# Attention beside a token-mixing MLP: where the last MLP products run, how wide token mixing's first weights are read, and how the first weights are loaded

## The chip, the cores and the metric

The kernel runs on one core of one Trainium2 chip. That core has a matrix engine (TensorE, "PE" in the profile, with its weight loads shown apart as "PEld"), a vector engine (VectorE, "DVE"), a scalar engine (ScalarE, "ACT"), GpSimd ("POOL"), and a sync engine (SyncE, "SP") that here only issues DMAs. Each engine works through its own queue in order; between engines there are semaphores. Matrix products land in PSUM, eight banks of 128 partitions by 512 fp32 numbers, and other engines carry them from there to SBUF.

The metric is device microseconds (us) for one execution, lower is better. A kernel's time is the median of its executions; one more execution is taken under the profiler, and its trace is what this document reads.

## What is computed

From the reference, cut to what matters (S = 2048 tokens, D = 448 features, H = 16 query heads of Dh = 28, one key and one value head, F = 1792):

```python
x = A_x
g = sigmoid((x * gate_w).sum(-1, keepdims=True))

# a: attention, 16 query heads on one key and one value head
q = (x @ wq) in 16 heads;  k = x @ wk;  v = x @ wv
p = softmax(q @ k.T * Dh ** -0.5)
a = concat_heads(p @ v) @ wo

# b: token mixing, then a channel-mixing MLP
h  = gelu(layernorm(x) @ w1)                # 448 -> 448
hs = the four quarters of h, shifted by +1, -1, +2, -2 tokens, @ w2
x1 = x + hs
b  = x1 + gelu(layernorm(x1) @ w3) @ w4     # 448 -> 1792 -> 448

out = g * a + (1 - g) * b
```

## The kernel before

**Stages.** The program runs in this order: (1) queries, keys, values and gate, as one product with the padded weights `wq` (512 columns), written to DRAM as `qd`; (2) token mixing, `stage_w1` and `stage_w2` for four blocks of 512 tokens; (3) the channel MLP, for each block 14 slices of 128 of the 1792 hidden features (`w3_part`, `w4_part`); (4) attention, for 16 units `u` (a block of 512 queries and four heads), each in eight stretches `v` of 256 keys, 128 stretches `k = 8u + v` in all; (5) a tail. Tiles and engines' orders are written by hand: each engine gets its instructions in the order of the Python code, so a line that is moved in the code moves in the queues.

**Accuracy by splitting.** A product in fp32 is made of products in a faster form (fp32r): weights and data are split in a high and a low part (`w1h`, `w1l`; `ah`, `al`), and high×high, high×low and low×high are added up in PSUM. In `proj` (L129 to L135) this makes 11 matmuls for the 448 input features: three chunks of 128 with three products each, and a last chunk with two.

**The start.** The scalar engine's queue issues the loads of `wqraw`, the sync queue those of the first block of `x` (`xkv_0`), both in four chunks of 128 features. Chunk 0 of `wqraw` comes in two DMAs, columns 0 to 127 and 128 to 511. Meanwhile PE runs 20 matmuls on zeros (L93). `first_queries` then takes chunk 0 of weights and data unsplit in fp32 (L312, four matmuls which the trace shows as eight passes), and chunks 1 to 3 in split form (L316), for which ACT casts `wqh` (L97) and DVE makes `wql` (L98).

**Token mixing's w1.** `stage_w1(b)` makes the four quarters of `h`, each with one `proj` call. The weights of quarter `m` are 112 columns, `w = slice(m * C, (m + 1) * C)` with `C = 112`, so that 112 of 128 PSUM partitions are written. DVE multiplies `ps[0:C]` by the layernorm factor, ACT applies gelu.

**The last MLP slice.** In the last block (tokens 1536 to 2047, x1 tiles n = 12 to 15), slice 13's products with `w4` are not made in the MLP. They are put off into attention: `last_g` holds the slice's gelu (`gh_late`, `gl_late`), and `w4_half` makes, for 128 tokens and 224 of 448 columns, three matmuls into one bank, whose sum DVE multiplies by `gi` (that is 1 - g) and adds to `x1`, which POOL has already multiplied by `gi` (`weigh_x1`, L642, in the POOL queue ahead of attention). There are eight halves, one in each of the stretches k = 3 to 10 (`W4_AT = 3`).

**A stretch of attention.** For stretch k, PE makes the scores of 2 × 128 keys (`scores`, L896: four heads side by side in the array's rows, 12 matmuls into four banks, twice). `exps` takes six of the eight banks by ACT (L920, exp from PSUM) and two by DVE (L917, a plain copy to `pd`); `late_exps` lets ACT do the exp of those two at once (L925). Then PE makes what is slotted in (a `w4_half`, or from the unit's fourth stretch on a `wo_half` of an earlier unit), and `values(k-1)` (L936: 32 matmuls into two banks), which DVE adds to `o`. Banks are handed out from a list in turn: `take` removes the first, and whoever has read a bank puts it at the end. A matmul that gets a bank waits until its last reader is done. One `values` lags one stretch behind the scores.

Of the kernel before, what the change touches and what calls it, by code (L numbers as in the profile page):

```python
# [42 lines left out]
def gated_mix_kernel(  # L43
# [85 lines left out]
    def proj(ps, wh, wl, ah, al):  # L129
        for c in range(3):  # L130
            nc.tensor.matmul(ps, wh[:, c, :], ah[:, c, :], start=(c == 0), stop=False)  # L131
            nc.tensor.matmul(ps, wh[:, c, :], al[:, c, :], start=False, stop=False)  # L132
            nc.tensor.matmul(ps, wl[:, c, :], ah[:, c, :], start=False, stop=False)  # L133
        nc.tensor.matmul(ps, wh[:, 3, :], ah[:, 3, :], start=False, stop=False)  # L134
        nc.tensor.matmul(ps, wl[:, 3, :], ah[:, 3, :], start=False, stop=True)  # L135
# [114 lines left out]
    with tc.tile_pool(name="s1b", bufs=1) as s1b, \  # L250
# [25 lines left out]
        wql = s1.tile([P, 4, 512], F32R, name="wql")  # L276
        xraw[0] = s1.tile([P, 4, 512], F32, tag="raw", bufs=3, name="xkv_0")
        for c in range(4):
            for cols in (slice(0, P), slice(P, 512)) if c == 0 else (slice(0, 512),):
                nc.scalar.dma_start(wqraw[:, c, cols], wq[:, c, cols])  # L280
            nc.sync.dma_start(xraw[0][:, c, :], xT[:, c, 0:512])
        nc.scalar.activation(first, powt, AF.Gelu_apprx_tanh)
        w1h = s1.tile([P, 4, D], F32R, name="w1h")
        w1l = s1.tile([P, 4, D], F32R, name="w1l")
        w2h = s1b.tile([P, 4, D], F32R, name="w2h")
        w2l = s1b.tile([P, 4, D], F32R, name="w2l")
        hh, hl, acts = {}, {}, {}
# [135 lines left out]
        def stage_w1(b, between=None):  # L423
# [6 lines left out]
                    nc.gpsimd.tensor_copy(tt[b][0:C, :, 0:2], f32(tt[b - 1])[0:C, :, 512:514])  # L430
            for i, m in enumerate(ORDER):
                ps = mm1(f"h_{b}_{m}")
                w = slice(m * C, (m + 1) * C)
                proj(ps[0:C, :], w1h[:, :, w], w1l[:, :, w], *xact[b])
                if between:
                    between(i)
                hf = s1.tile([P, 512], F32, tag="hf", bufs=3, name=f"hf_{b}_{m}")
                nc.vector.tensor_mul(hf[0:C, :], ps[0:C, :], rb_of[b][0:C, :])
                nc.scalar.activation(hh[b][0:C, m, 2:514], hf[0:C, :], AF.Gelu_apprx_tanh)
                nc.scalar.activation(hf[0:C, :], hf[0:C, :], AF.Gelu_apprx_tanh)  # L440
                nc.gpsimd.tensor_tensor(hl[b][0:C, m, 2:514], hf[0:C, :], f32(hh[b])[0:C, m, 2:514],
                                        ALU.subtract)
                if i == 1:
                    carry_h(b)
# [50 lines left out]
        centre_w1()  # L495
        stage_q(7)
        stage_q(8)
        split_w_high(w1raw, w1h, w1l)
        for t in range(4):
            ln1_tile(1, t)  # L500
        split_w_low(w1raw, w1h, w1l)
        stage_q(9)
        ln1_send(0)
        ln1_read(0)
# [248 lines left out]
    with tc.tile_pool(name="s3", bufs=1, reuse_waits="tile") as s3, \  # L753
# [77 lines left out]
            t, h = divmod(i, 2)  # L831
            wo_job(u, t, None, slice(224 * h, 224 * h + 224))

        weigh_x1(NT - 4, NT)

        def w4_half(i):
            t, h = divmod(i, 2)
            n = NT - 4 + t
            cols = slice(224 * h, 224 * h + 224)
            tok = slice(t * P, (t + 1) * P)  # L840
            gh, gl = last_g
            ps = bank(f"job_{n}_{h}")[:, cols]
            nc.tensor.matmul(ps, gh[:, tok], w4h[-1][:, 1, cols], start=True, stop=False)
            nc.tensor.matmul(ps, gh[:, tok], w4l[-1][:, 1, cols], start=False, stop=False)
            nc.tensor.matmul(ps, gl[:, tok], w4h[-1][:, 1, cols], start=False, stop=True)
            nc.vector.scalar_tensor_tensor(x1[:, n, cols], ps, gi[:, n:n + 1], x1[:, n, cols],
                                           op0=ALU.mult, op1=ALU.add)

        def redo_unit(i, acc, gd):
            b, g = i // NG, i % NG  # L850
# [95 lines left out]

        READ = (0, 3, 1, 2)
        DRAIN = 3
        W4_AT = 3

        for k in range(NU * NV):
            u, v = divmod(k, NV)
# [6 lines left out]
            for kt in (2 * v, 2 * v + 1):  # L959
                exps(u, kt, scores(u, kt))  # L960
            late_exps(u, v)
            if 0 <= k - W4_AT < 8:
                w4_half(k - W4_AT)
            if v >= 4 and u:
                wo_half(u - 1, v - 4)
            if v < 4 and u > 1:
# [156 lines left out]
```

## Time and profile before

| | before |
|---|---|
| median of 3 executions | 922.65 us (922.6 to 924.09) |
| the profiled execution's own time | 921.51 us |
| its span in the trace | 919.7 us |
| granted TensorE clock, mean | 0.998 |
| PE busy | 910.3 us, 99% of the span |
| ACT busy | 634.8 us, 69% |
| DVE busy | 543.7 us, 59% |
| POOL busy | 104.9 us, 11% |

The profiled execution's time is 1.8 us above the span, which is what lies around the instructions, and 1.1 us under the median. "Busy" counts an instruction from start to end; matmuls overlap each other, so a busy PE is not one at its peak, and what a matmul costs is read from the distance between starts. In a timeline row, the first number is the start in us from the span's start, the second the duration, then engine, line, operation, output<-input, shape and count; in brackets stands the idle time ahead of it and what ended that.

### The profile page before, as it was taken

The page shows a single profiled execution, that of the slowest core. Times are in us where ns is not written, and L with a number is a line of the kernel's source. Part 1 is how long each engine was busy: PE and PEld are TensorE (multiplying, and loading weights), DVE is VectorE, ACT ScalarE, POOL GpSimd, SP SyncE. Part 2 cuts the span into 40 slices and gives each one's busy share as a digit, 9 for nine tenths or more (in the row PEclk, how much of TensorE's full clock was granted, in tenths as well). Part 3 has the DMA queues.
Part 4 walks back from the last instruction along what each step waited for, and adds up shares of the span by engine and source line. Part 5 has one row for each costly group of instructions (what it writes and reads, how often), then busy time and mean ns, then how long its engine had stood idle before and what let it go on. Part 6 is the DMA issues. An engine that isn't in the chain of part 4 may idle for free.

```text
span 919.7 us, 24031 instructions
## 1 busy us (share of the span) xinstructions
PE 910.3 (99%) x10051; PEld 646.7 (70%) x10051; DVE 543.7 (59%) x1085; ACT 634.8 (69%) x1134; POOL 104.9 (11%) x135
## 2 busy tenths in 40 slices
PE   9999999999999999999999999999999999999997
PEld 6788888888888888875655665666665556666563
DVE  4675264631435746446666766666667666676664
ACT  5542255322222131259999999999999999999994
POOL 2143200221000530031000000000000000000000
PEclk9999999999999999999999999999999999999999
DMA  8821543220222132110100001000011000110001
GB/s 289 301 77 43 165 144 118 40 66 21 41 69 50 33 97 65 28 55 22 26 26 2 26 14 55 25 26 26 10 39 46 26 4 25 35 45 3 14 14 43
DMA packets 41953, 51.82 MB, mean 56 GB/s; under 512 B 9328, under 2 KB 27824, under 8 KB 41840
## 3 DMA queue, kind: packets, MB, share of 16 engines
q1 hardware_dynamic: 38672, 44.77, 17.0%
q10 hardware_dynamic: 3168, 5.47, 1.7%
q8 instruction: 80, 1.31, 0.6%
q14 instruction: 33, 0.27, 0.1%
HBM read 37.04 MB, written 11.93 MB: 53 GB/s over the span
## 4 chain that ended last, share of the span: by engine, by line
PE 96%; ACT 1%; DMA 1%; DVE 0%; issue 0%; ACTq 0%; DVEq 0%
PE bank L936 23%; PE bank L896 22%; PE bank L816 7%; PE acc L678 5%; PE acc L677 5%; PE acc L679 5%; PE g L132 4%; PE g L131 4%; PE g L133 4%; PE hs L456 1%; PE hs L457 1%; PE g L134 1%; PE g L135 1%; PE h L131 1%; PE h L132 1%; PE h L133 1%
## 5 line engine op out<-in xcount | busy, mean ns | idle before, releaser
L920 ACT ACTIVATE p<-bank 128x512 f32<-128x512 f32 x768 | 390.2, 619 | 4.8 <-PE bank L896 4.4
L936 PE MATMUL bank<-p,vext 128*32 128x256 f32 x3072 | 243.9, 379 | 0.8 <-ACT p L920 0.8
L936 PE MATMUL bank<-pd,vext 128*32 128x256 f32 x1024 | 242.2, 379 | 0.3 <-ACT pd L925 0.3
L917 DVE COPY pd<-bank 128x512 f32<-128x512 f32 x256 | 176.5, 691 | 53.2 <-PE bank L896 52.1
L936 PEld LDWEIGHTS bank<-p,vext 128*32 128x32 f32 x3072 | 125.1, 110 | 82.3 <-ACT p L920 2.1
L667 ACT ACTIVATE gh<-g 128x512 fp32r<-128x512 f32 x55 | 32.8, 597 | 186.7 <-PE g L135 186.7
L941 DVE TENSOR_TENSOR o<-o,bank 128x256 f32<-128x256 f32 x222 | 93.4, 421 | 91.4 <-ACT p L920 49.9
L925 ACT ACTIVATE pd<-pd 128x1024 f32<-128x1024 f32 x128 | 142.2, 1111 | 0.0
L896 PE MATMUL bank<-qh,kH 30*128 30x512 f32 x1024 | 119.8, 444 | 0.0
L936 PEld LDWEIGHTS bank<-pd,vext 128*32 128x32 f32 x1024 | 111.6, 110 | 1.3 <-ACT pd L925 0.7
L669 DVE TENSOR_TENSOR gl<-gf,gh 128x512 fp32r<-128x512 f32 x55 | 37.9, 688 | 123.7 <-ACT gf L668 123.7
L896 PE MATMUL bank<-qh,kL 28*128 28x512 f32 x1024 | 106.2, 394 | 0.0
L896 PE MATMUL bank<-ql,kH 28*128 28x512 f32 x1024 | 105.6, 389 | 0.0
L896 PEld LDWEIGHTS bank<-qh,kH 30*128 30x128 f32 x1024 | 61.0, 182 | 58.2 <-ACT p L920 47.0
L678 PE MATMUL acc<-w4l,gh 128*128 128x448 f32 x220 | 80.4, 366 | 0.0
L677 PE MATMUL acc<-w4h,gh 128*128 128x448 f32 x220 | 80.3, 365 | 0.0
L679 PE MATMUL acc<-w4h,gl 128*128 128x448 f32 x220 | 80.1, 364 | 0.0
L816 PE MATMUL bank<-wof,on 128*32 128x224 f32 (+1 forms) x992 | 73.1, 370 | 0.3 <-ACT p L920 0.3
L132 PE MATMUL g<-al,w3h 128*128 128x512 f32 x168 | 65.8, 392 | 0.0
L131 PE MATMUL g<-ah,w3h 128*128 128x512 f32 x168 | 65.6, 391 | 0.0
L133 PE MATMUL g<-ah,w3l 128*128 128x512 f32 x168 | 65.5, 390 | 0.0
L896 PEld LDWEIGHTS bank<-ql,kH 28*128 28x128 f32 x1024 | 52.6, 185 | 8.2
(196 smaller groups left out, 1165.2 us busy)
## 6 DMA issues: line engine op xcount, KB each, us to landing
qd<-qf ACTq DMA_DIRECT2D x16, 256.0 KB
qm<-qd SPq DMA_DIRECT2D x16, 256.0 KB
qr<-qd SPq DMA_DIRECT2D x16, 256.0 KB
rb<-rd SPq DMA_DIRECT2D x15, 256.0 KB
x<-in_x_dram SPq DMA_DIRECT2D x4, 896.0 KB
xd<-xt SPq DMA_DIRECT2D x16, 224.0 KB
w34raw<-in_w_dram SPq DMA_DIRECT2D x7, 512.0 KB
out_dram<-ot SPq DMA_DIRECT2D x15, 224.0 KB
```

Source lines behind the costliest of these rows:

```text
L131: nc.tensor.matmul(ps, wh[:, c, :], ah[:, c, :], start=(c == 0), stop=False)
L132: nc.tensor.matmul(ps, wh[:, c, :], al[:, c, :], start=False, stop=False)
L133: nc.tensor.matmul(ps, wl[:, c, :], ah[:, c, :], start=False, stop=False)
L677: nc.tensor.matmul(ps, gh[:, tok], w4h[i][:, k, :], start=(f == 0), stop=False)
L678: nc.tensor.matmul(ps, gh[:, tok], w4l[i][:, k, :], start=False, stop=False)
L679: nc.tensor.matmul(ps, gl[:, tok], w4h[i][:, k, :], start=False, stop=(f == stop))
L816: nc.tensor.matmul(ps[32 * j:32 * j + 32, cols], on_of[u][:, tok], wof[:, g, cols], start=True, stop=True, tile_position=(0, 32 * j))
L896: nc.tensor.matmul(bs[j], w, a, start=(i == 0), stop=(i == 2), tile_position=(32 * j, 0))
L917: nc.vector.tensor_copy(ps[j], bs[j])
L920: behind[kt % 2] = nc.scalar.activation(ps[j], bs[j], AF.Exp, scale=SCALE)
L925: ins = nc.scalar.activation(pd, pd, AF.Exp, scale=SCALE)
L936: nc.tensor.matmul(pv[32 * j:32 * j + 32, q], vext[:, kt, :], p_of[u, kt][j][:, q], start=(kt % 2 == 0), stop=(kt % 2 == 1), tile_position ...
```

## The change

```diff
@@ loads of the first weights
         for c in range(4):
-            for cols in (slice(0, P), slice(P, 512)) if c == 0 else (slice(0, 512),):
-                nc.scalar.dma_start(wqraw[:, c, cols], wq[:, c, cols])
+            nc.scalar.dma_start(wqraw[:, c, :], wq[:, c, :])
             nc.sync.dma_start(xraw[0][:, c, :], xT[:, c, 0:512])
         nc.scalar.activation(first, powt, AF.Gelu_apprx_tanh)
-        w1h = s1.tile([P, 4, D], F32R, name="w1h")
-        w1l = s1.tile([P, 4, D], F32R, name="w1l")
+        w1h = s1.tile([P, 4, D + P - C], F32R, name="w1h")
+        w1l = s1.tile([P, 4, D + P - C], F32R, name="w1l")
+        for w in (w1h, w1l):
+            nc.gpsimd.memset(f32(w)[:, :, D:D + P - C], 0.0)
@@ stage_w1
-                w = slice(m * C, (m + 1) * C)
-                proj(ps[0:C, :], w1h[:, :, w], w1l[:, :, w], *xact[b])
+                w = slice(m * C, m * C + P)
+                proj(ps, w1h[:, :, w], w1l[:, :, w], *xact[b])
@@ the split of w1
-        split_w_high(w1raw, w1h, w1l)
+        split_w_high(w1raw, w1h[:, :, 0:D], w1l[:, :, 0:D])
...
-        split_w_low(w1raw, w1h, w1l)
+        split_w_low(w1raw, w1h[:, :, 0:D], w1l[:, :, 0:D])
@@ attention
-        weigh_x1(NT - 4, NT)
-
-        def w4_half(i):
-            t, h = divmod(i, 2)
+        def w4_job(t):
             n = NT - 4 + t
-            cols = slice(224 * h, 224 * h + 224)
             tok = slice(t * P, (t + 1) * P)
             gh, gl = last_g
-            ps = bank(f"job_{n}_{h}")[:, cols]
-            nc.tensor.matmul(ps, gh[:, tok], w4h[-1][:, 1, cols], start=True, stop=False)
-            nc.tensor.matmul(ps, gh[:, tok], w4l[-1][:, 1, cols], start=False, stop=False)
-            nc.tensor.matmul(ps, gl[:, tok], w4h[-1][:, 1, cols], start=False, stop=True)
-            nc.vector.scalar_tensor_tensor(x1[:, n, cols], ps, gi[:, n:n + 1], x1[:, n, cols],
-                                           op0=ALU.mult, op1=ALU.add)
+            ps = bank(f"job_{n}")[:, 0:D]
+            nc.tensor.matmul(ps, gh[:, tok], w4h[-1][:, 1, :], start=True, stop=False)
+            nc.tensor.matmul(ps, gh[:, tok], w4l[-1][:, 1, :], start=False, stop=False)
+            nc.tensor.matmul(ps, gl[:, tok], w4h[-1][:, 1, :], start=False, stop=True)
+            nc.vector.tensor_add(x1[:, n, :], x1[:, n, :], ps)
...
-        W4_AT = 3
...
             late_exps(u, v)
-            if 0 <= k - W4_AT < 8:
-                w4_half(k - W4_AT)
+            if k == 0:
+                for t in range(3):
+                    w4_job(t)
+            if k == 1:
+                w4_job(3)
+                weigh_x1(NT - 4, NT)
```

So there are three edits. Chunk 0 of `wqraw` comes in one DMA in place of two. Each quarter of `w1` is read with the 16 columns behind it (the next quarter's, or, for the last, zeros that POOL writes once), and the 16 extra rows of the result are not used. The eight half jobs of stretches 3 to 10 become four whole jobs, three in stretch 0 and one in stretch 1; their sums are added to `x1` unweighted, and POOL's weighting of these four tiles comes after them.

How this moves the engines' queues, at three places. On ACT, the queue's head (loads of `wqraw` are issued from here), before:

```order
L280 DMA wqraw<-in_wq_dram 128x128
L280 DMA wqraw<-in_wq_dram 128x384
L280 DMA wqraw<-in_wq_dram 128x512 x3
L282 ACT_TABLE_LOAD
L282 ACTIVATE first<-powt 128x4
```

and with the change:

```order
L279 DMA wqraw<-in_wq_dram 128x512 x4
L281 ACT_TABLE_LOAD
L281 ACTIVATE first<-powt 128x4
L122 CAST ahk_145<-xkv_120 128x512
L97 CAST wqh<-wqraw 128x512
```

One issue fewer stands ahead of the table load and the first casts. On PE, at the start of attention, from the end of the second set of scores (`kH` and `kL` are the keys' parts, `qh` and `ql` the queries', a bank's number is its tile), before:

```order
L896 MATMUL bank_3508<-ql_1030,kH 128x512
L896 MATMUL bank_3509<-ql_1030,kH 128x512
L896 MATMUL bank_3502<-qh_1029,kH 128x512
L896 MATMUL bank_3505<-qh_1029,kH 128x512
L896 MATMUL bank_3503<-qh_1029,kH 128x512
L896 MATMUL bank_3504<-qh_1029,kH 128x512
```

and with the change:

```order
L892 MATMUL bank_3509<-ql_1031,kH 128x512
L892 MATMUL bank_3510<-ql_1031,kH 128x512
L840 MATMUL bank_3503<-w4h_1480,gh_late 128x448
L841 MATMUL bank_3503<-w4l_1481,gh_late 128x448
L842 MATMUL bank_3503<-w4h_1480,gl_late 128x448
L840 MATMUL bank_3506<-w4h_1480,gh_late 128x448
L841 MATMUL bank_3506<-w4l_1481,gh_late 128x448
L842 MATMUL bank_3506<-w4h_1480,gl_late 128x448
L840 MATMUL bank_3504<-w4h_1480,gh_late 128x448
L841 MATMUL bank_3504<-w4l_1481,gh_late 128x448
L842 MATMUL bank_3504<-w4h_1480,gl_late 128x448
L892 MATMUL bank_3505<-qh_1030,kH 128x512
```

The nine matmuls of three jobs stand between the second and the third set of scores; the jobs take the three banks that come free first (of the first scores' heads 0, 3 and 1), and the third scores begin with the next. On DVE, at the same place, with the change (before, the four rows of L843 are not here; eight rows of L846, one a stretch, follow later):

```order
L913 COPY pd_3533<-bank_3506 128x512
L913 COPY pd_3533<-bank_3510 128x512
L843 TENSOR_TENSOR x_72<-x_72,bank_3503 128x448
L843 TENSOR_TENSOR x_72<-x_72,bank_3506 128x448
L843 TENSOR_TENSOR x_72<-x_72,bank_3504 128x448
L913 COPY pd_3534<-bank_3508 128x512
L913 COPY pd_3534<-bank_3504 128x512
L843 TENSOR_TENSOR x_72<-x_72,bank_3505 128x448
```

The adds of three jobs stand between the copies of the first and of the second stretch. On POOL the four weightings of `x1` keep their place in the order, ahead of the split of unit 1's queries, but now wait for these adds.

## The prediction

> **What bounds the kernel now.** I read the page first (busy shares, then the chain of waits), then busy time by windows at the places that the change touches, then the timelines there.
>
> ```profile
> PE 910.3 (99%) x10051; PEld 646.7 (70%) x10051; DVE 543.7 (59%) x1085; ACT 634.8 (69%) x1134; POOL 104.9 (11%) x135
> PE 96%; ACT 1%; DMA 1%; DVE 0%; issue 0%; ACTq 0%; DVEq 0%
> core 0: us, PE busy (x) PEld busy (x) DVE busy (x) ACT busy (x) POOL busy (x), PEclk, DMA share, GB/s
> 0.00:5.20 5.20, 4.15 (x20) 2.97 (x21) 0.17 (x1) 0.41 (x1) 2.50 (x14) 1.00 0.62 161
> 37.50:58.00 20.50, 20.50 (x91) 15.41 (x91) 13.02 (x19) 12.59 (x21) 7.73 (x8) 1.00 0.55 170
> 404.40:415.85 11.45, 10.65 (x144) 6.23 (x144) 5.92 (x11) 11.44 (x22) 5.56 (x6) 1.00 0.42 130
> 415.85:448.33 32.48, 32.16 (x476) 19.69 (x472) 21.01 (x42) 32.05 (x57) 3.69 (x4) 1.00 0.07 16
> ```
>
> PE is 99% busy and 96% of the chain that ended last. Token mixing (37.5 to 58) has no PE gap: what PE saves there comes off the end. In attention two engines are full at once: from 404.4 to 415.85 ACT is busy for 11.44 of 11.45 us and PE is not, from 415.85 to 448.33 both nearly. So each stage has its own price, and I take the three edits in the order in which they run.
>
> **First weights whole.**
>
> ```profile
> 0.73 4.03 ACTq L280 DMA_DIRECT2D wqraw<-in_wq_dram  x5
> 5.08 0.33 PEld L312 LDWEIGHTS q<-xkv,wqraw 128*128 128x128 f32 x2
> 6.28 0.30 PEld L312 LDWEIGHTS q<-xkv,wqraw 128*128 128x128 f32 x2 [0.88 <-DMA wqraw<-in_wq_dram]
> 7.67 0.19 PEld L312 LDWEIGHTS q<-xkv,wqraw 128*128 128x128 f32 x1 [0.24 <-issue]
> 8.10 0.19 PEld L312 LDWEIGHTS q<-xkv,wqraw 128*128 128x128 f32 x1 [0.24 <-issue]
> 8.55 0.62 ACT L97 CAST wqh<-wqraw 128x512 fp32r<-128x512 f32 x1 [1.75 <-DMA wqraw<-in_wq_dram]
> 9.22 0.77 PEld L316 LDWEIGHTS q<-ahk,wqh 128*128 128x128 f32 x4 [0.93 <-ACT wqh L97]
> ```
>
> The eight fp32 passes step by 0.43 us (7.67 to 8.10). Two run on the narrow piece, then PE stands until the other 384 columns are there at 6.28. The last pass begins at 8.53 and would let PE go on at 8.96; but chunk 1 lands only at 8.55, and PE resumes at 9.22. Now the issues are one fewer, so chunks 1 to 3 are asked for earlier. Does chunk 0 make it by 5.2, when PE's warm-up ends? By the window's row 161 GB/s × 5.2 us = 837 KB are in by then; chunk 0 of weights and of data are 2 × 262 = 524 KB, and both are first in their queues. I take yes. Then eight passes run without a stop, 5.2 + 8 × 0.43 + 0.05 = 8.7, and chunk 1, asked for one issue earlier, is cast by then. Gain 9.22 − 8.7 = 0.5 us. The other end: the whole chunk lands when the second piece did, 6.28 + 8 × 0.43 + 0.1 = 9.82, a loss of 0.6. Behind this PE is without gaps, so either passes through.
>
> **w1 in 128 columns.** 16 quarters × 11 = 176 matmuls, each with its load.
>
> ```profile
> L131 PEld LDWEIGHTS h<-ahk,w1h 128*112 128x112 f32 x48 | 8.4, 174 | 2.7 <-issue 0.2
> L131 PEld LDWEIGHTS q<-ahk,wqh 128*128 128x128 f32 x36 | 6.8, 188 | 1.7 <-issue 0.2
> 16.65 0.39 PE L131 MATMUL q<-ahk,wqh 128*128 128x512 f32 x1
> 24.13 0.91 PE L397 MATMUL wsum_ps<-wsum,ones 128*128 128x448 f32 x2
> 25.12 0.40 PE L132 MATMUL q<-alk,wqh 128*128 128x512 f32 x1
> 27.43 0.39 PE L131 MATMUL q<-ahk,wqh 128*128 128x512 f32 x1
> 47.83 0.39 PE L131 MATMUL h<-ahk,w1h 128*112 128x512 f32 x1
> 57.96 0.37 PE L456 MATMUL hs<-w2h,hh 112*128 112x448 f32 x1
> 67.11 0.39 PE L131 MATMUL h<-ahk,w1h 128*112 128x512 f32 x1
> 77.32 0.27 PE L375 MATMUL rsT<-ident,rs_s 128*4 128x128 f32 x1
> ```
>
> The narrow load is shorter (174 against 188 ns), and yet its matmuls are further apart. Queries, 128 columns: 33 matmuls from 16.65 to 24.13, 226.7 ns each. w1, 112 columns: 44 from 47.83 to 57.96, 230.2 ns; 44 from 67.11 to 77.32, 232.0 ns. The pair 25.12 and 27.43 shows how: after a foreign matmul (L397) the 128-wide stream too runs at 231 ns for ten matmuls, and then is back at 227; the 112-wide one stays off. If the width is what lets it settle, the two shown stages save 10.13 − 9.97 and 10.21 − 9.97, 0.40 us; the four, 0.8. Some 0.1 goes to settling behind token mixing's w2 products and a transpose in the first stage: 0.7. The bounds: nothing, if it is not the width but that these slices begin every 112 columns, which they still do (hence no gain); and a loss of 176 × (188 − 174) = 2.5 us, if the longer load is not covered. It is covered now: 188-ns loads run under matmuls 227 apart. POOL's two memsets run in the first microseconds, far ahead of w1.
>
> The Trainium skill ("TensorE: Matmul & The Clock Gate", LDWEIGHTS) says that a load's time goes with its columns, and (Part 3) that a load overlaps running matmuls only in another row group. The first agrees with 174 and 188 ns; by the second the 2.5 us would be paid, while here a 188-ns load fits between starts 227 ns apart that leave no room for both in turn. That is a rival below.
>
> **Whole jobs at the head of attention.**
>
> ```profile
> 399.06 0.36 PE L677 MATMUL acc<-w4h,gh 128*128 128x448 f32 x1
> 403.11 0.36 PE L679 MATMUL acc<-w4h,gl 128*128 128x448 f32 x1
> 403.40 0.50 PE L896 MATMUL bank<-qh,kH 30*128 30x512 f32 x4
> 405.06 1.47 PE L896 MATMUL bank<-qh,kH 30*128 30x512 f32 x4
> 428.82 0.37 PE L843 MATMUL bank<-w4h,gh_late 128*128 128x224 f32 x1
> 429.35 0.42 PE L936 MATMUL bank<-p,vext 128*32 128x256 f32 x3
> 447.35 0.51 PE L896 MATMUL bank<-qh,kH 30*128 30x512 f32 x4
> 448.99 0.42 PE L936 MATMUL bank<-p,vext 128*32 128x256 f32 x3
> 450.85 0.51 PE L896 MATMUL bank<-qh,kH 30*128 30x512 f32 x4
> 404.41 3.04 ACT L920 ACTIVATE p<-bank 128x512 f32<-128x512 f32 x6 [3.37 <-PE bank L896]
> 408.23 3.10 ACT L920 ACTIVATE p<-bank 128x512 f32<-128x512 f32 x6
> 412.04 3.16 ACT L920 ACTIVATE p<-bank 128x512 f32<-128x512 f32 x6
> 415.85 3.23 ACT L920 ACTIVATE p<-bank 128x512 f32<-128x512 f32 x6
> 452.16 3.10 ACT L920 ACTIVATE p<-bank 128x512 f32<-128x512 f32 x6
> L749 DVE TENSOR_TENSOR x<-x,acc 128x448 f32<-128x448 f32 x4 | 2.4, 621 | 0.2 <-PE acc L679 0.2
> ```
>
> Removed: a half costs PE 429.35 − 428.82 = 0.53 us. A stretch without any (k = 11) is 1.64 of scores and 1.86 of values, 3.50; with a half it is 4.03, which is over what ACT needs: without halves ACT starts a stretch every 3.82 us (404.41, 408.23, 412.04, 415.85). So stretches 3 to 10 are paced by PE, and from 415.85 to 452.16 nine stretches take 36.31 us. At ACT's pace they take 34.38: a gain of 1.93. At k = 12 PE is ahead of ACT as before, and what follows is unchanged.
>
> Added: a job is three matmuls of 448 columns, 0.2025 us apart (20 steps from 399.06 to 403.11), 0.61. The first can start at 405.06, when ACT has read the first bank (there the third scores start now). Three end at 406.9. The third scores then have their exp input 1.01 us later (403.40 to 404.41), at 407.95: before 408.23, so ACT loses nothing. Three DVE adds of 0.62 follow the copies and end near 407.85, which lets the fourth scores go at 407.9; PE is done with them near 408.8. The fourth job needs a bank that ACT reads from 408.23 for some 0.6: it runs from 408.9 to 409.5, values until 411.4, and the next scores give their exp input at 412.4, where ACT wants 412.04. Lost: 0.35. Afterwards PE gains 0.3 a stretch. Net 1.9 − 0.35 = 1.6 us. Bounds: 1.9 if ACT waits nowhere; a loss of 0.5, if all four jobs fall on ACT (4 × 0.61 = 2.4).
>
> POOL's weighting now ends some 5 us later; behind it in the queue stand unit 1's queries, needed only at stretch 8, 20 us on. DVE has 1.0 us less to do.
>
> **Sum.** 0.5 + 0.7 + 1.6 = 2.8 us, on the profiled execution 921.51 → 918.7. The median shown is 922.65, so 919.8.
>
> **Rivals.** *Jobs fall on ACT* (0.12): each bank handed back late by DVE, the attention part at +0.5; in all −0.7, 921.9. For it: DVE's copies stand behind three adds. Against: the fourth scores' exp input is there at 408.9, and ACT, three exps of 0.48 into its stretch (six take 408.23 − 404.41 less the 0.95 of the late exp), wants it at 409.7. *Width is not the cause* (0.12): −2.1, 920.5. For it: the start of the slices. Against: the settling of L131's queries. *Chunk 0 late* (0.09): +0.6 in place of −0.5, −1.7, 920.9. For it: the second piece, asked for 0.4 us later, came at 6.28. Against: it shared its turn with narrow packets. *Loads uncovered* (0.04): +2.5 in place of −0.7, +0.4, 923.0. *The slower side* (0.05): the chunk on which all of PE's start hangs comes as late as chunk 1 came, 8.5. From 5.2 PE idles, resumes chunk 1 at 12.0 rather than 9.22, +2.8; and if the clock, granted at 1.00 in all windows shown, then falls, the eight passes at half speed cost 3.4 more: 6.2 − 0.7 − 1.6 = +3.9, 926.5. It decides from a landing near 8.5, a gap of 3.3 us, three times the 1.1 us shown ahead of 6.28. In the Trainium skill's account (same page, Part 1) the clock falls after a full idle window of about 3.4 us, which bears the small chance out; no row here shows a fall.
>
> **Numbers.** The forecast has 0.58. What a measurement of this kernel tells from no change is about 0.2%, 1.85 us: faster means below 920.8. Faster: 0.55 of the forecast, 0.09 of the width rival, 0.06 of the borderline ones, 0.70. Slower 0.06, the rest 0.24. Range: 918.6 (all bounds on the good side, −3.3, and a median 0.7 lower) to 922.0 (jobs on ACT). The forecast's own: 919.0 to 920.8.
>
> **What would show it.** L312 at eight even steps from 5.2 and L316 at 8.7; w1 stages of about 10.0 us; ACT's stretches 3 to 11 at 3.82 and one near 4.2 early. Wrong it is if L312 starts near 6.3, if w1's matmuls stay 231 apart, or if ACT idles in stretches 1 and 2 for more than 1 us.

## The result, and the profile after

The changed kernel takes 920.98 us (median of 16 executions, 919.58 to 922.21), the kernel before, in the same session, 922.47 us (16 executions, 920.9 to 924.09). The ratio is 0.9983, with a 95% interval of 0.9975 to 0.9990: 1.5 us faster, between 0.9 and 2.3. The forecast was 2.8 us, and 919.8.

The page's busy line of the changed kernel: PE has 2.6 us less to do than the 910.3 us of before, and is still full.

```profile
PE 907.7 (99%) x10039; PEld 646.3 (70%) x10039; DVE 543.0 (59%) x1081; ACT 634.6 (69%) x1134; POOL 105.4 (11%) x137
```

The profiled execution itself took 921.3 us with a span of 919.5 us, only 0.2 less than the 919.7 of before. Three edits and one stall make that up, and each is read at its own place.

**The start**, timelines of the changed kernel, PEld's (the weight loads) and then PE's (start, duration, line, shapes, count):

```profile
5.18 0.41 PEld L313 LDWEIGHTS q<-xkv,wqraw 128*128 128x128 f32 x2 [0.17 <-DMA wqraw<-in_wq_dram]
5.83 0.19 PEld L313 LDWEIGHTS q<-xkv,wqraw 128*128 128x128 f32 x1 [0.24 <-issue]
...
7.97 0.19 PEld L313 LDWEIGHTS q<-xkv,wqraw 128*128 128x128 f32 x1 [0.24 <-issue]
```

```profile
8.43 1.50 PE L317 MATMUL q<-ahk,wqh 128*128 128x512 f32 x4
...
16.14 0.39 PE L131 MATMUL q<-ahk,wqh 128*128 128x512 f32 x1
```

The eight passes follow each other without the wait for a transfer that the kernel before had at 6.28. The first product of the next queries comes at 16.14; before it came at 16.65. So this execution is 0.51 us ahead of that one here; the experiments ask how much of this is the edit's.

**Token mixing's w1**, the first matmul of one stage and the first behind it, in the same timeline:

```profile
47.35 0.39 PE L131 MATMUL h<-ahk,w1h 128*128 128x512 f32 x1
...
57.55 0.37 PE L457 MATMUL hs<-w2h,hh 112*128 112x448 f32 x1
```

The loads are 128 wide now, and 44 matmuls still take 10.20 us, 231.8 ns each (230.2 and 232.0 in the two stages of before that the prediction showed). Over all 16 products of 11 matmuls the mean is 2.553 us after and 2.551 before: nothing is saved.

**A stall that was not there before**, in the third part of token mixing (all engines' timeline, in brackets the idle time and what ended it):

```profile
116.53 2.18 ACT L611 CAST ah<-xr 128x512 fp32r<-128x512 f32 x4 [7.90 <-DMA xr<-xd]
117.18 1.30 DVE L614 TENSOR_TENSOR al<-xr,ah 128x512 fp32r<-128x512 f32 x2 [2.87 <-ACT ah L611]
117.81 0.37 PE L460 MATMUL hs<-w2h,hl 128*128 128x448 f32 x1
118.40 0.61 DVE L462 TENSOR_TENSOR x<-x,hs 128x448 f32<-128x448 f32 x1
119.06 0.47 PE L457 MATMUL hs<-w2h,hh 112*128 112x448 f32 x1 [0.89 <-DVE x L462]
```

Read it from the bottom: PE at 119.06 waits for an add on DVE (L462) that hands a bank back. The add stands in DVE's queue behind two subtractions (L614), these wait for ACT's casts (L611), and the casts for a read from DRAM (`xr<-xd`) that landed near 116.5. From 117.81 to the next matmul are 1.25 us where 0.20 is usual: 1.05 us lost. That is why this one execution is hardly faster than the one of before; the medians are further apart.

**Attention**, ACT's timeline of the changed kernel, one row for the six bank exps of a stretch:

```profile
405.14 3.05 ACT L916 ACTIVATE p<-bank 128x512 f32<-128x512 f32 x6 [3.37 <-PE bank L892]
408.97 3.09 ACT L916 ACTIVATE p<-bank 128x512 f32<-128x512 f32 x6
413.34 3.05 ACT L916 ACTIVATE p<-bank 128x512 f32<-128x512 f32 x6 [0.34 <-PE bank L892]
417.18 3.09 ACT L916 ACTIVATE p<-bank 128x512 f32<-128x512 f32 x6
420.99 3.15 ACT L916 ACTIVATE p<-bank 128x512 f32<-128x512 f32 x6
...
447.87 3.41 ACT L916 ACTIVATE p<-bank 128x512 f32<-128x512 f32 x6
451.73 3.42 ACT L916 ACTIVATE p<-bank 128x512 f32<-128x512 f32 x6
```

The starts of stretches 3 to 8 are 3.82 us apart as forecast, but those from 8 to 12 are 3.88 apart, and stretch 1 takes 4.37. From the start of stretch 0 to that of stretch 13 it is 50.85 us, against 51.70 before: 0.85 saved, not 1.6. Sum for this execution: −0.51, +0.04 for w1, +1.05 and −0.85 are −0.27; the spans differ by −0.2.

Look at the durations in these rows as well. They grow: 3.05, 3.09, 3.15, up to 3.42. The same was so in the rows of before (3.04, 3.10, 3.16, 3.23). What that means was the question of the experiments.

### The profile page after: what moved, and what is told of

The parts are those of the page before. It is cut to its first block, busy times and chain, and to the rows that moved or that the text cites. A ratio compares the mean times of both kernels' runs of the same rounds, so it can differ in the third digit from the quotient of the medians.

```text
span 919.5 us, 24000 instructions
## 1 busy us (share of the span) xinstructions
PE 907.7 (99%) x10039; PEld 646.3 (70%) x10039; DVE 543.0 (59%) x1081; ACT 634.6 (69%) x1134; POOL 105.4 (11%) x137
## 3 DMA queue, kind: packets, MB, share of 16 engines
q10 hardware_dynamic: 3024, 5.47, 1.7%
## 5 line engine op out<-in xcount | busy, mean ns | idle before, releaser
L921 ACT ACTIVATE pd<-pd 128x1024 f32<-128x1024 f32 x128 | 144.1, 1125 | 0.0
L892 PE MATMUL bank<-qh,kH 30*128 30x512 f32 x1024 | 117.5, 444 | 0.0
L131 PE MATMUL g<-ah,w3h 128*128 128x512 f32 x168 | 65.6, 391 | 0.0
```

What stands on the lines that cost most here:

```text
L892: nc.tensor.matmul(bs[j], w, a, start=(i == 0), stop=(i == 2), tile_position=(32 * j, 0))
L921: ins = nc.scalar.activation(pd, pd, AF.Exp, scale=SCALE)
```

## The experiments

Twelve kernels in four sessions, each session with its own runs of the kernel before. Ratios are to those, with 95% intervals. "k = 0 to 13" is the time from the start of ACT's stretch 0 to that of stretch 13 in the profiled execution. The column on the clock counts the executions whose mean granted TensorE clock was 0.997 or less.

| kernel | median us | ratio | k = 0 to 13 | low clock |
|---|---|---|---|---|
| before (84 runs in four sessions) | 922.4 to 923.1 | | 51.70 | 35 of 84 |
| the changed kernel | 920.98 | 0.9983 (0.9975 to 0.9990) | 50.85 | 0 of 16 |
| e1: first edit alone | 921.62 | 0.9991 (0.9982 to 1.0000) | 52.68 | 7 of 11 |
| e2: second edit alone | 922.32 | 0.9998 (0.9989 to 1.0008) | 51.71 | 4 of 11 |
| e3: third edit alone | 920.62 | 0.9981 (0.9972 to 0.9990) | 50.86 | 0 of 11 |
| e4: changed, w1 every 128 columns | 919.43 | 0.9971 (0.9961 to 0.9981) | 50.84 | 0 of 9 |
| e5: e4 read 112 wide | 920.37 | 0.9977 (0.9967 to 0.9988) | 50.85 | 0 of 8 |
| e6: e4 moved by 16 columns | 920.99 | 0.9984 (0.9975 to 0.9993) | 50.85 | 0 of 11 |
| e7: e4 without jobs | 919.77 | 0.9976 (0.9967 to 0.9985) | 50.41 | 2 of 11 |
| e8: e4, fourth job behind the values | 920.39 | 0.9976 (0.9966 to 0.9986) | 50.85 | 0 of 9 |
| e9: e4 with half of the first values products | one execution | | 49.89 | 0 of 1 |
| e10: before, with idle time filled | 921.77 | 0.9994 (0.9985 to 1.0003) | 51.68 | 0 of 11 |
| e11: e4 with later splits | 919.07 | 0.9961 (0.9948 to 0.9975) | 50.84 | 0 of 5 |
| e12: changed, with later splits | 919.80 | 0.9968 (0.9956 to 0.9980) | 50.83 | 0 of 6 |

### The three edits one by one (e1, e2, e3)

e1 is the kernel before with this edit:

```diff
-            for cols in (slice(0, P), slice(P, 512)) if c == 0 else (slice(0, 512),):
-                nc.scalar.dma_start(wqraw[:, c, cols], wq[:, c, cols])
+            nc.scalar.dma_start(wqraw[:, c, :], wq[:, c, :])
```

> The kernel before with the first edit alone: chunk 0 of the first weights in one transfer. Theory A (the changed kernel's trace: L316's equivalent, the first matmul on split weights, begins 0.5 to 0.8 us earlier and nothing on PE absorbs it before the end): -0.5 us, a ratio near 0.9995, with the first stage-2 query matmul at 16.1 rather than 16.65. Rival B (the half microsecond is eaten later, by a transfer that now comes too late for PE, as the changed kernel's trace has a gap of 1.05 us at 117.8 in the third part of token mixing, on the read of the normalised x): 0 to +0.5 us, and the same gap near 118 in this kernel's trace.

Measured: 0.8 us below before, with an interval from 0 to 1.7, so it agrees with A but can't be told from nothing by itself. In its trace the eight passes run from 5.14 without a stop, the next queries begin at 15.92, and PE has no gap near 118: the stall does not follow from an earlier start alone. But its stretch 1 takes 4.92 us; e10 comes back to that. Seven of its eleven executions have the low clock of the table, against 10 of 31 of before beside it. Among the executions with a low clock the means are 922.04 and 922.85 us, among the others 921.22 (only four) and 922.23, so it is some 0.8 to 1.0 us ahead in both groups.

The other profiles say less. Three more kernels load chunk 0 in two transfers: e2, e3 and e10. In them, too, PE waits for the second piece between its passes, for 1.39, 0.50 and 1.04 us, and yet their next queries begin at 16.20, 16.12 and 16.08. From e3's timelines:

```profile
6.08 0.36 PEld L312 LDWEIGHTS q<-xkv,wqraw 128*128 128x128 f32 x2 [0.50 <-DMA wqraw<-in_wq_dram]
8.44 0.19 PEld L316 LDWEIGHTS q<-ahk,wqh 128*128 128x128 f32 x1 [0.28 <-ACT wqh L97]
16.12 0.39 PE L131 MATMUL q<-ahk,wqh 128*128 128x512 f32 x1
```

Chunk 1 is ready for PE at 8.39 to 8.79 in these three and at 9.22 in the profile of before, which was a late one. In the ten profiles with the edit the next queries begin at 15.89 to 16.30, 16.08 on average, in the four without it at 16.08 to 16.65, 16.26 on average. That is 0.2 us, with ranges that overlap. The wait between the passes is gone in all ten; whether that is worth 0.2 us or the 0.8 of e1's runs stays open.

e2 is before with 128-wide slices of `w1` (the second and third hunk of the diff).

> The kernel before with the second edit alone: w1's quarters read 128 columns wide, still every 112 columns. Theory A (width does not matter): 0.0 us, an h product of 11 matmuls at 2.55 us as before, matmuls 231 to 232 ns apart. Rival B (width matters, as forecast): -0.7 us, products at 2.50 us. Rival C (the longer load costs something where it isn't covered): up to +0.5 us, products above 2.56.

Measured: ratio 0.9998, products of 2.553 us on average. A holds, B is out, and C too: the 188-ns loads cost nothing, so the Trainium skill's rule that the prediction weighed ("TensorE: Matmul & The Clock Gate", Part 3) doesn't charge its 2.5 us here.

e3 is before with the four whole jobs in stretches 0 and 1 (the last two hunks).

> The kernel before with the third edit alone: the last MLP products as four whole jobs at the head of attention. Theory A (the lead theory: without halves ACT runs at 3.82 us a stretch only while PE's scores are more than 1.0 us ahead of it, and that lead shrinks by 0.06 us a stretch, because PE waits twice a stretch for banks that ACT reads): -0.85 us, stretches near 3.88 from about the eighth on, and one of 4.26 where the first output half comes in. Rival B (the forecast: ACT's pace for all of them): -1.6 us. Rival C (the loss is of the changed kernel's one profile only): about -1.2 us and no stretch at 3.88 ahead of the output halves.

Measured: k = 0 to 13 in 50.86 us against 51.70, stretches at 3.88 from the eighth on and 4.26 at k = 12. These are the numbers of A, but e7 and e9 show that A had the wrong cause for them. The median gain, 1.8 us (0.9 to 2.6), is more than the 0.85 of the profiles; e10 gives a reason for a part of the rest.

### What keeps w1's matmuls 231 ns apart (e4, e5, e6)

e4 is the changed kernel with room for 128 columns for each quarter (cut to what matters; `w1l` is treated alike):

```diff
-        w1h = s1.tile([P, 4, D + P - C], F32R, name="w1h")
+        w1h = s1.tile([P, 4, 512], F32R, name="w1h")
...
-                w = slice(m * C, m * C + P)
+                w = slice(m * P, m * P + P)
```

> The changed kernel with w1's quarters kept every 128 columns (16 zero columns behind each) and read 128 wide from there; ACT and DVE write the quarters with the same number of instructions. Theory A (the slices' start decides: a load that begins off a 512-byte step is what keeps the matmuls 231 ns apart): h products of 11 matmuls at 2.50 us in place of 2.55, 16 of them, so -0.8 us against the changed kernel, which is -2.3 against the kernel before. Rival B (neither width nor start, but what the products follow or read beside the weights): 2.55 us, no change against the changed kernel (-1.5 against before). Rival C (the strided writes of the split weights are slower and hold PE): slower than the changed kernel.

e5 is e4 with `w = slice(m * P, m * P + C)` and `ps[0:C, :]` as before.

> As e4 (quarters of w1 every 128 columns), but read 112 columns wide from there, as the kernel before did from its 112-column steps. Theory A (the start of the slices alone decides): h products of 11 matmuls at 2.493 us, matmuls 227 ns apart, as e4, and the time of e4: -2.9 us against before. Rival B (it takes both, 128 columns and the start): products at 2.55 us, matmuls 231 apart, 0.8 us above e4.

e6 is e4 with the tile begun 16 columns earlier, so that what is read begins 64 bytes off:

```diff
-        w1h = s1.tile([P, 4, 512], F32R, name="w1h")
+        w1h = s1.tile([P, 16 + 2048], F32R, name="w1h")[:, 16:].rearrange("p (c n) -> p c n", c=4)
```

> As e4, 128 columns wide and a step of 128 columns, but the whole tile moved by 16 columns, so that each slice begins 64 bytes off a 512-byte step. Theory A (the start against 512 bytes decides): matmuls back at 231 ns, products at 2.55 us, 0.8 us above e4. Rival B (what hurt was that neighbouring quarters shared bytes or that their step was odd): 227 ns and 2.493 us as e4.

PE's timelines, the same stage as above (first matmul, and first one behind it). e4:

```profile
46.92 0.39 PE L131 MATMUL h<-ahk,w1h 128*128 128x512 f32 x1
...
56.89 0.36 PE L461 MATMUL hs<-w2h,hh 112*128 112x448 f32 x1
```

e5:

```profile
47.04 0.39 PE L131 MATMUL h<-ahk,w1h 128*112 128x512 f32 x1
...
57.11 0.36 PE L461 MATMUL hs<-w2h,hh 112*128 112x448 f32 x1
```

e6:

```profile
47.74 0.39 PE L131 MATMUL h<-ahk,w1h 128*128 128x512 f32 x1
...
57.89 0.37 PE L461 MATMUL hs<-w2h,hh 112*128 112x448 f32 x1
```

Forty-four matmuls take 9.97 us in e4 (226.6 ns each), 10.07 in e5 (228.9) and 10.15 in e6 (230.7), against 10.20 in the changed kernel. Over all 16 products: 2.505, 2.524 and 2.545 us against 2.553, that is 0.8, 0.5 and 0.1 us saved. So the place where a slice starts decides most of it, and the width then counts too: 128 columns at the wrong start gain nothing (e2), 112 at a good start gain 0.5, 128 at a good start all 0.8. Neither theory of e5 is right as it stood; the truth lies between. e6 shows that a step of 512 bytes between slices is not enough when their start is off by 64 bytes. Which starts would do, other than a multiple of 512 bytes from the tile's start, was not tried. The medians of the three follow this order, but their intervals overlap; the traces tell them apart.

### ACT's pace (e7, e8, e9)

e7 is e4 with the jobs left out:

```diff
-            if k == 0:
-                for t in range(3):
-                    w4_job(t)
             if k == 1:
-                w4_job(3)
                 weigh_x1(NT - 4, NT)
```

> As e4, but the four whole jobs and their adds left out, so that the last MLP slice is missing from four tiles of x1: the floor for any place of the jobs. Theory A (ACT itself takes 3.88 us a stretch, read from the ends of its exps, 407.45, 411.33, 415.20, 419.08 in the kernel before; starts 3.82 apart only run ahead of the ends until they can't): starts 3.82 apart for the first eight or so, then 3.88, ends 3.875 apart throughout, still 4.26 at k = 12; from k = 0 to k = 13 50.3 us rather than e4's 50.84, so -0.5 against e4 in an undisturbed profile. Rival B (the jobs use up a lead of PE, and 3.88 comes from there): 3.82 up to k = 11, 49.9 us, -0.9 against e4. Beside that, the fall of the granted clock at the head of attention: in the kernel before 10 of 31 runs had a mean clock of 0.996, in the ones with whole jobs none of 36. If it is PE's idle time in stretch 1 that lets it fall, it is back here in a third of the runs; if it was the halves, it stays away.

ACT's timeline of e7:

```profile
403.62 3.04 ACT L920 ACTIVATE p<-bank 128x512 f32<-128x512 f32 x6 [3.37 <-PE bank L896]
407.44 3.10 ACT L920 ACTIVATE p<-bank 128x512 f32<-128x512 f32 x6
411.25 3.17 ACT L920 ACTIVATE p<-bank 128x512 f32<-128x512 f32 x6
...
445.89 3.42 ACT L920 ACTIVATE p<-bank 128x512 f32<-128x512 f32 x6
449.77 3.41 ACT L920 ACTIVATE p<-bank 128x512 f32<-128x512 f32 x6
```

Add duration to start: the last exp of stretch 0 ends at 406.66, that of stretch 1 at 410.54, of stretch 2 at 414.42, of stretch 11 at 449.31. That is 42.65 us for eleven stretches, 3.877 each, and the first ones are no quicker than the last. The starts, 3.82 apart at first, run ahead of the ends until the lead is some 0.4 us, and from then on (3.88 from about stretch 6) keep their pace. With no job in the way at all, starts still fall back to 3.88: A holds, with 50.41 us where 50.3 was expected, and B, the lead theory of e3, falls. It also gives the price of the jobs, 50.84 − 50.41 = 0.43 us, and no place for them can gain more than that in this span.

The Trainium skill ("Perfetto Trace Analysis", DVE / Act Engine Instruction) says that an ACT row runs from the start of execution to the acknowledgement of the last write, and that the next instruction may begin sooner. The rows agree: the next stretch's first exp begins while the last row of the one before is open, and the row's end, not its start, is when others may go on. That the overlap grows from stretch to stretch is not in it; that is these rows alone.

e9 takes work from PE and leaves ACT's as it is:

```diff
-                for kt in (2 * v, 2 * v + 1):
+                half = 8 * u + v < 12
+                for kt in (2 * v,) if half else (2 * v, 2 * v + 1):
...
```

> As e4, but in the first twelve stretches the values products take only the first 128 of each stretch's 256 keys, so that half of these products is left out and PE has 0.9 us less to do in a stretch; ACT has the same exps. Theory A (3.88 us is what ACT itself needs for a stretch): from k = 3 to 11 the ends of ACT's last bank exp stay 3.875 apart, and the starts come to 3.88 as in e4; from k = 0 to 13 about e7's 50.4 us, since no place is left where PE is late. Rival B (3.88 is a loop through PE: values, scores, exp): ends 3.82 apart or closer, starts 3.82 up to k = 11. PE stands idle more here, so the granted clock may fall in places; only ACT's spacing is read from this run.

ACT's timeline of e9, and under it the start of its values products in three stretches, from PE's:

```profile
406.95 3.10 ACT L920 ACTIVATE p<-bank 128x512 f32<-128x512 f32 x6
410.76 3.17 ACT L920 ACTIVATE p<-bank 128x512 f32<-128x512 f32 x6
...
445.03 3.79 ACT L920 ACTIVATE p<-bank 128x512 f32<-128x512 f32 x6
448.83 3.86 ACT L920 ACTIVATE p<-bank 128x512 f32<-128x512 f32 x6
```

```profile
430.91 0.42 PE L937 MATMUL bank<-p,vext 128*32 128x256 f32 x3 [0.46 <-ACT p L920]
434.79 0.42 PE L937 MATMUL bank<-p,vext 128*32 128x256 f32 x3 [0.46 <-ACT p L920]
438.66 0.42 PE L937 MATMUL bank<-p,vext 128*32 128x256 f32 x3 [0.45 <-ACT p L920]
```

The starts stay 3.81 apart up to stretch 12 and the row gets longer and longer, to 3.86 us. The ends: 410.05 in stretch 1, 452.69 in stretch 12, 42.64 us for eleven stretches, 3.876 each, the same as in e7. PE, which waits for ACT in each of these rows, moves on every 3.88 us too. So 3.876 us is what ACT itself needs for a stretch in this kernel: it is the same with no jobs and with half of the values products, no row of ACT waits for another engine from stretch 1 to 12 in either, and it is the ends that the others feel. One detail of A was wrong: starts don't have to come back to 3.88 at any fixed lead, here it grew to 0.82 us (3.86 − 3.04). The 49.89 us of this kernel is therefore no gain over e7; by ends, stretch 0 to stretch 13 takes 50.39 us here and 50.41 there.

e8 moves the fourth job, in Python, behind `values(0)` in stretch 1.

> As e4, but the fourth whole job stands behind the values of stretch 0 (in stretch 1) and not ahead of them. Theory A (the 4.36 at k = 1 to 2 comes of the fourth job, which holds PE before values that ACT's next input waits behind; without the job there PE has 0.8 us to spare): that stretch 3.9, k = 0 to 13 50.4 us, -0.45 against e4. Rival B (the loss comes of the three jobs in stretch 0, since the fourth job's bank and its neighbours are late by DVE's adds): still 4.3 to 4.4, no change against e4. If PE's idle time ahead of those values lets the clock fall, some runs are at 0.996 again.

ACT's stretch 1 in e8, and PE's timeline from there to the next scores:

```profile
408.75 3.09 ACT L920 ACTIVATE p<-bank 128x512 f32<-128x512 f32 x6
```

```profile
409.44 0.42 PE L936 MATMUL bank<-p,vext 128*32 128x256 f32 x3
...
409.68 0.39 PE L936 MATMUL bank<-p,vext 128*32 128x256 f32 x3
...
409.90 0.39 PE L936 MATMUL bank<-p,vext 128*32 128x256 f32 x3
...
411.31 0.47 PE L844 MATMUL bank<-w4h,gh_late 128*128 128x448 f32 x1
411.61 0.37 PE L845 MATMUL bank<-w4l,gh_late 128*128 128x448 f32 x1
411.82 0.37 PE L846 MATMUL bank<-w4h,gl_late 128*128 128x448 f32 x1
412.12 0.51 PE L896 MATMUL bank<-qh,kH 30*128 30x512 f32 x4
```

Stretch 1 takes 4.37 us as before the move, so A's number is missed. The rows say why, and it isn't B's reason either: the values wait until 409.44, for ACT's first exp of the stretch, begun at 408.75, and then 1.87 us of values, 0.81 of job and the scores follow without a stop. Without the job the scores would begin at 411.3 and give ACT its input near 412.3, 1.0 us later; ACT's next stretch is due 3.81 us after 408.75, at 412.56. The room is 0.2 to 0.3 us, not 0.8, and a job of 0.8 overruns it on either side of the values. That the values wait for that exp is no effect of the three jobs: in the kernel before, without any job there, they begin 0.70 us behind it as well (408.93 and 408.23).

```profile
408.93 0.42 PE L936 MATMUL bank<-p,vext 128*32 128x256 f32 x3 [0.46 <-ACT p L920]
```

### The clock at the head of attention (e1 again, and e10)

The windows view of e1's profile (PE, PEld, DVE, ACT and POOL busy, then the granted clock, DMA share, GB/s), and two rows of its PE timeline there:

```profile
404.00:408.30 4.30, 3.87 (x36) 1.97 (x28) 2.38 (x4) 4.30 (x9) 3.38 (x3) 0.94 0.83 274
408.30:411.40 3.10, 3.07 (x32) 1.38 (x32) 0.73 (x2) 3.10 (x6) 1.50 (x2) 0.54 0.03 7
```

```profile
409.19 0.65 PE L935 MATMUL bank<-p,vext 128*32 128x256 f32 x3
...
409.61 0.65 PE L935 MATMUL bank<-p,vext 128*32 128x256 f32 x3
```

For 3 us the granted clock is 0.54, and the values products step by 0.42 us where e8's step by 0.22 (409.68 to 409.90). That is the 4.92 us of e1's stretch 1 and its 52.68 us. In narrower windows the clock is 0.50 from about 407.75 to 411.15, 3.4 us. Over a span of 920 us this takes 0.0019 off the mean clock, which is 0.996 in this execution. Only the mean clock is listed for every run: in the kernel before 35 of 84 have 0.997 or less, and they are 0.6 to 1.0 us longer than the others in each of the four sessions (0.8 weighted by runs). That their clock falls at this place too is taken from e1, the only profile of such an execution. In the profiles shown of before and after the clock there is 1.00, so none of this could be read from them.

e10 is the kernel before with nine more matmuls in stretch 0 whose result nothing reads:

```diff
+            if k == 0:
+                for t in range(3):
+                    gh, gl = last_g
+                    ps = bank(f"fill_{t}")[:, 0:D]
+                    tok = slice(t * P, (t + 1) * P)
...
             if 0 <= k - W4_AT < 8:
                 w4_half(k - W4_AT)
```

> The kernel before, with three more jobs of three matmuls in stretch 0, where the changed kernel has its own, whose sums nothing reads; the eight halves stay in stretches 3 to 10. It makes more work and only fills PE's idle time ahead of stretch 1. Theory A (part of what the whole jobs gain is that PE is no longer idle for 0.85 us around 408, where the granted clock falls to 0.54 for 3 us in some executions of the kernel before, 25 of 59 runs at a mean clock of 0.996): no run at 0.996, and the median 0.3 to 0.4 us below before although no work is taken out; stretches as in before otherwise, 51.7 us from k = 0 to 13. Rival B (the falls belong to the halves or to chance): 0.996 in some four of ten runs as before, and the time of before or a little above.

The same windows of e10:

```profile
404.00:408.30 4.30, 4.20 (x45) 2.84 (x37) 1.98 (x3) 4.30 (x9) 3.38 (x3) 1.00 0.86 277
408.30:411.40 3.10, 3.06 (x52) 2.01 (x56) 1.64 (x5) 3.10 (x6) 1.21 (x2) 1.00 0.01 3
```

No run of eleven has a low clock, 8 of 15 of the kernel before beside it have. Over all kernels with jobs or filling in stretch 0 it is 0 of 87; with neither, and with the halves, 46 of 106 (before, e1 and e2); with neither and without the halves, 2 of 11 (e7). That settles that filling stretch 0 keeps the clock up; e7 speaks against the halves as the cause, since its clock falls without them. The gain in the median, 0.6 us, has an interval from −0.3 to 1.4, so its size is better estimated from the counts: 35/84 × 0.8 = 0.3 us.

The Trainium skill ("TensorE: Matmul & The Clock Gate", Part 1) lets the clock fall after a full idle window of about 3.4 us. No such window stands at the fall in e1: PE's longest idle time from 404.00 to 408.33 is 0.46 us. But the 3.87 of 4.30 us that PE counts as busy there flatter it, because a matmul's row can contain its wait for a bank: from 404.46 to 408.33, 3.87 us, PE makes one stretch's scores, which are 1.64 us of work. The same page's section "A second HAM failure mode: psum-queue depth-cycling", in which PE is idle for short spells between groups of matmuls that cycle through PSUM banks, fits this place better: PE's waits here are for banks that ACT reads. Which share of idle time lets the clock fall, no run here shows.

### The stall in token mixing (e11, e12)

e11 is e4, and e12 is the changed kernel itself, with this edit:

```diff
-            elif t > 1:
-                ln_split(0, 2 * t - 4, 2 * t - 2)
+            elif t == 3:
+                ln_split(0, 0, 2)
...
         def weights(t):
+            if t == 0:
+                ln_split(0, 2, 4)
```

> As e4, with the first splits of the read-back x moved behind one more product tile (third part of token mixing and the one after it), so that DVE's add that hands back an hs bank no longer stands behind them. The profiles of after, of e5 and of e8 have a PE gap of 1.0 to 1.6 us at 117 to 118, where that read takes 7.9 to 8.5 us from issue to landing; the others, with 6.3 to 7.1 us, have none. Theory A (a chance of the transfer's landing, in about three of ten executions): no gap, a narrower spread, and a median equal to e4's or up to 0.4 us below. Rival B (the splits are then late for the next stage, whose first products wait for them): a PE gap of up to 2 us near 128 and a time above e4's.

> The changed kernel itself, with only the first splits of the read-back x moved behind one more product tile, as in e11. Its own profile has a PE gap of 1.05 us there, and its sixteen runs spread from 919.58 to 922.21. Theory A (the gap comes by chance of the transfer in some of the executions and costs the changed kernel some 0.3 to 0.5 us of its median): no gap, runs within 1 us of each other, the median 0.3 to 0.5 us below the changed kernel's, a ratio to before of 0.9979. Rival B (the spread and the gap have nothing to do with each other, or the splits moved later cost as much elsewhere): the changed kernel's ratio, 0.9983, and its spread.

DVE's timeline of e12 at this place:

```profile
115.93 0.62 DVE L462 TENSOR_TENSOR x<-x,hs 128x448 f32<-128x448 f32 x1 [1.64 <-PE hs L460]
116.71 1.29 DVE L614 TENSOR_TENSOR al<-xr,ah 128x512 fp32r<-128x512 f32 x2 [0.15 <-ACT ah L611]
118.19 0.62 DVE L462 TENSOR_TENSOR x<-x,hs 128x448 f32<-128x448 f32 x1 [0.19 <-PE hs L460]
```

The tile's add now stands ahead of the subtractions, and the next one waits for PE rather than PE for it. PE has no gap there in either profile, nor near 128. The runs come closer together: 919.40 to 920.57 in e12 (six), 918.82 to 919.38 in e11 (five), where the changed kernel had 919.58 to 922.21 and e4 919.08 to 921.65. So both go A's way, if with few executions: e11's median is 0.36 us below e4's, and e12's runs are 1.2 us apart where at most 1 was expected. e12's ratio is 0.9968 against 0.9983 for the changed kernel, 1.4 us, more than the 0.3 to 0.5 expected, with intervals that overlap, so the size is not settled. The stall was in the profiles of the changed kernel, e5 and e8 (1.05 to 1.6 us), where ACT stands idle for 7.9 to 8.5 us until the read has landed, and not in e1, e4, e6, e7 and e9 with the same order of splits, where this wait is 6.3 to 7.1 us. In the profiles of e11 and e12 it is 6.9 and 7.5 us, so they don't show the new order under a wait as long as in the stalls. None of the four profiles without the first edit (before, e2, e3, e10) has it. That is too few to say whether the earlier start makes it likelier, and this stays open.

e11 is the quickest kernel of the study that computes everything: 919.07 us, 3.6 us under before (2.3 to 4.8), under the changed kernel as well.

## Why the prediction was half right

**First weights whole: the mechanism right, the size open.** L316 was to begin at 8.7 and its successor L317 began at 8.43. Chunk 0 was there by 5.05 to 5.47 in all ten profiles with this edit, so neither the "chunk 0 late" rival nor the slower side came about. But "Gain 9.22 − 8.7 = 0.5" takes its 9.22 from one execution, and in the three other profiles with two transfers PE goes on at 8.39 to 8.79. That the pair of profiles shows 0.51 is therefore in part luck: the profiles together give 0.2 us, e1's runs 0.8 (0 to 1.7). The clock did fall in this study, but elsewhere: at the head of attention, in kernels without work in stretch 0.

**w1 in 128 columns: the wrong cause.** The step that failed is "if the width is what lets it settle", taken at 0.7 us with 0.12 for the rival that it is not. The pair of L131 queries showed that 128-wide products settle back to 227 ns; but those queries also begin on multiples of 128 columns, so the pair could not tell width from start. The term's own lower bound named it, "that these slices begin every 112 columns", and e4, e5 and e6 show that this was the larger part: 0 of 0.8 us at the old start, 0.5 from the start alone, 0.8 from both. By its own sign, "if w1's matmuls stay 231 apart", the forecast was wrong here: they stayed 231.8 apart. The rival "Width is not the cause" came true.

**Whole jobs at the head of attention: the mechanism right, two sizes off.** Stretches with halves are paced by PE, those without by ACT, as forecast. The failed step is "At ACT's pace they take 34.38": that pace, 3.82 us, was read from the starts of ACT's rows. By their ends it is 3.876, and the rows quoted for the 3.82 held it: 404.41 + 3.04, 408.23 + 3.10, 412.04 + 3.16 and 415.85 + 3.23 are 3.87 to 3.88 apart. By ends, the eight stretches with halves took 419.08 to 451.38, 32.30 us, and now take 420.27 to 451.28, 31.01: 1.3 us gained instead of 1.93. The fourth job costs 4.33 − 3.88 = 0.45 us by ends instead of 0.35, since it takes 0.81 us with its waits (e8's rows) and not 0.61. Net 0.85. The 4.26 us at k = 12 in the starts (4.25 to 4.26 in e3, e4 and e7), which the forecast did not have, costs nothing: the ends around it are 3.87 to 3.90 apart, before and after, and only the lead of the starts is given back.

**Two things were not in the sum.** The whole jobs keep the clock up in the executions where it fell, worth an estimated 0.3 us on average and not visible in the one profile of before, whose clock held. And the changed kernel has a stall of 1.05 to 1.6 us in some of its executions (three of the eight profiles that have the first edit and the old order of splits, 0.46 us on average over these). With both, and 0.2 to 0.8 us for the start, the sum is −0.9 to −1.5 us: −0.85 − 0.33 + 0.46 = −0.72, and the start. The measured 0.9 to 2.3 us hold that, but do not settle the start's part.

**Jobs fall on ACT** did not happen, and loads stayed covered. The range held the result, partly by luck: of 2.8 us forecast, w1's 0.7 did not come and the jobs gave 0.85 in place of 1.6, while a gain of 0.3 from the clock, which no term foresaw, made up for a part. The result lies at 0.17%, just short of what was called faster.

## What to carry to other kernels

Take an engine's pace from the ends of its rows where others wait for its results, and be wary when durations of equal instructions grow: the starts are running ahead. When two streams differ in width, look whether they also differ in where their slices begin, and test one at a time; here weights padded to a step of 128 columns were worth 0.8 us that reading wider was not. And one profile is one execution: look at the mean clock and the spread of all runs, and at the same place in the profiles of other kernels that share it, before a gain is booked to the cause that a single pair of traces shows.

## What was not expected of the hardware

- ACT began equal stretches 3.81 us apart while finishing them 3.876 us apart, for twelve stretches on end (e9), with the six bank exps of a stretch recorded ever longer (3.04 to 3.86 us).
- Matmuls with 128×512 data were 227 ns apart with weights of 128 columns at multiples of 512 bytes in their tile, 229 with 112 columns there, and 230 to 232 with either width at the 448-byte steps.
- The granted clock fell to 0.5 for 3.4 us (e1) although PE was not idle for more than 0.46 us at a time in the 4 us around its start; it had 1.64 us of work in 3.87 us there. A mean clock as low as in that execution came in 35 of 84 executions of the kernel before, and with nine more matmuls in that place in none of eleven.
